# GpSimd issues the later gathers, and two more blocks of the second feed-forward load their float64 weights directly

## The chip, the cores and the metric

The program runs on one core of one Trainium2 chip. The number that counts is the device time of one execution in microseconds (us), here the median of a few runs. The core has five engines with an instruction stream each: TensorE (PE), VectorE (DVE), ScalarE (ACT), GpSimd (POOL) and SyncE (SP). SP and POOL issue the kernel's DMA transfers, each in the order of its own stream; the data are moved by 16 DMA engines which both share.

## The reference

Three stages stand one behind the other, on 1536 tokens of 384 features:

```python
# 1. gated linear attention: 2 batches, 8 heads of 48, 768 positions
state = alpha[t][:, None] * state + outer(k[t], v[t])
y[t] = q[t] @ state
# 2. top-1 mixture of experts: E = 8, F = 1024, capacity 384 rows each
expert_idx = argmax(x @ w_gate); gate_w = softmax(...)[expert_idx]
y = relu(disp @ w1[e]) @ w2[e]          # disp: the rows sent to expert e
out[i] = gate_w[i] * y[expert_idx[i], pos[i]]
# 3. second feed-forward, d_ff = 2048, weights w_in and w_out in float64
h = x @ w_in
g = h * tanh(softplus(h))
out = g @ w_out
```

## The kernel before

**Attention and routing** (0 to about 80 us). Twelve tiles of 128 tokens. At the very start SP loads the operands of the first tiles: `load_an` (L420) brings alpha, `load` (L443) brings q, k, v. Each finished tile is routed, and POOL scatters its rows into the table `tab` in DRAM (`scatter`, L108), at the place of their expert. The last two tiles are scattered last. They are also put together for expert 0 by matmuls: `slot_rest` (L834) adds for each of two chunks of rows (`CH`: 128 and 112) what expert 0's gather brought, and `route_rank_mm` stands between the two chunks.

**The experts** (82 to 223 us). The loop runs over 8 experts `e` and 8 blocks `m` of 128 hidden features: 64 steps of `g1` (L1047), and `g2` (L1064) of an earlier step. Three matmuls (high times high, low times high, high times low) make each product nearly exact in single precision, so each weight piece `st` from DRAM is split on the chip: ACT copies it to `whi` (L336), DVE subtracts to get `wlo` (L342). A piece is a block of one of the two matrices. The rows of expert e+1 are brought by `gather(e + 1)` (L124), two DMAs of 128 and 112 rows, into `xs`, which has one buffer. `xpose` (L1019) reads them by PE at m = 5 of expert e, and right behind it in the program stands the next gather. SP's queue carries the gathers, all weight pieces, and the conversion's loads and stores, one behind the other; an entry whose condition isn't met holds all behind it.

**The float64 weights.** While the experts run, 17 conversion jobs turn the weights of the first MA = 10 of 16 blocks of the second feed-forward into single precision. A job is a load of 64-bit words into `w64` (L222), an ACT square and check (L195, L230) and two DVE bit operations (`cvt_a`), a DVE join (`cvt_b`, L206) and a store to DRAM (L238), into `wi_s` or `wo_s`. Their halves lie evenly over 45 free steps (`job_at`). Later the weights are read back as pieces `st64` and on (`load_to`, L324), and `written(i)` names the jobs that must be done before a piece is loaded. The other 6 blocks are "late": `late_load` brings the 64-bit words directly (`sd`, L265 and L267), and ACT and DVE turn them into `whi` and `wlo` in some eight operations spread over the steps (`late_size`, `late_join`, `late_high`, `late_low`).

**The second feed-forward** (211 to 421 us). `f1` (L1127) and `f2` (L1170) run over 48 steps: first 10 blocks times three windows of 512 tokens, then 6 blocks times three. `f_mish(n)` has the activation, from PSUM (`sigma`, L1139 and L1143), and the sine tables (L1145), on ACT, then DVE's part. The first three steps (`EARLY`) overlap with the last three of the experts. The last piece conversions of that stretch, `conv_to`, stand on ACT behind `sigma(0)`.

Instructions on one engine run in the written order; the framework puts in the waits.

Of the kernel before, what the change touches and what calls it, by code (L numbers as in the profile page):

```python
# [10 lines left out]
F32 = mybir.dt.float32  # L11
# [12 lines left out]
def kernel(  # L24
# [18 lines left out]
    nc = tc.nc  # L43
# [3 lines left out]
    E = w1.shape[0]  # L47
# [11 lines left out]
    MF = FF // 128  # L59
    MF2 = FF2 // 128  # L60
    WIN = 240
    WB = 256
    CH = [(c, min(128, WIN - c)) for c in range(0, WIN, 128)]
    XW = NT + WIN
    PW = 768
# [13 lines left out]
    wst = main.enter_context(tc.tile_pool(name="wst", bufs=WST))  # L79
# [16 lines left out]
    tab = dram.tile([E * NT, DM], F32, name="tab")  # L96
# [23 lines left out]
    def gather(e):  # L120
        xs = xs_t[e] = xsp.tile([128, len(CH), DM], F32, tag="xs", name="xs")
        for c, n in CH:
            r0_ = (E - 1 - e) * NT + c
            r = nc.sync.dma_start(out=xs[0:n, c // 128, :], in_=tab[r0_:r0_ + n, :])  # L124
            for ins in free_rows["tab"]:
                tc.add_manual_dep(
                    r.ins, ins.name, mybir.DependencyInfo(mybir.DependencyClass.Sync, mybir.DependencyReason.DATA), reason="rows"
                )
# [30 lines left out]

    CN = 512  # L160
    MA = 10
    FH = MA * 128
    cvt_jobs = []
    wi_s = dram.tile([DM, FH], F32, name="wi_s")
    wo_s = dram.tile([FH, DM], F32, name="wo_s")
# [88 lines left out]


    late_t = {}
    NLATE = 2 * (MF2 - MA)

    def late_load(n):
        if not 0 <= n < NLATE:  # L260
            return
        st = wst.tile([128, PW], F32, tag="st", name=f"sd{n}")
        fs = slice(FH + n // 2 * 128, FH + (n // 2 + 1) * 128)
        if n % 2:
            nc.sync.dma_start(out=words(st), in_=words(w_out[fs, :]))  # L265
        else:
            nc.sync.dma_start(  # L267
                out=st.bitcast(U32).rearrange("p (k f) -> p k f", k=KD),
                in_=w_in.bitcast(U32)[:, 2 * fs.start:2 * fs.stop].rearrange("(k p) f -> p k f", p=128),
            )  # L270
        late_t[n] = st


    def late_size(n):
        if 0 <= n < NLATE:
            w = wst.tile([128, PW], F32, tag="st", name="sw")
            wt, wm = w[:, 0:DM].bitcast(U32), w[:, DM:2 * DM]
            late_t[n] = words(late_t[n]), wt, wm
            cvt_size(late_t[n][0][:, :, 1], wm)
# [6 lines left out]

    def late_at(n):
        wm = late_t[n][2]
        i = E * NP1 + (MA + n // 2) // 2 * 2 + n % 2
        if n // 2 % 2 == 0:  # L290
            if i == 76:
                early.close()
                wr_p.append(main.enter_context(tc.tile_pool(name="wr2", bufs=4, side="right")))
            w_new(i)
        if n % 2:
            hi, lo = w_second(E, MA + n // 2)
            w = wm
        else:
            hi, lo = w_first(E, MA + n // 2)
            w = wm.rearrange("p (k f) -> p k f", k=KD)  # L300
        return hi, lo, w

# [46 lines left out]
    def w_first(e, m):  # L349
        i = NP1 * e + m // 2 * 2  # L350
        return [w[i].rearrange("p (k f) -> p k f", k=KD)[:, :, m % 2 * 128:(m % 2 + 1) * 128] for w in (whi, wlo)]

    def w_second(e, m):
        i = NP1 * e + m // 2 * 2 + 1
        return [w[i][:, m % 2 * DM:(m % 2 + 1) * DM] for w in (whi, wlo)]


    with ExitStack() as actx:
# [58 lines left out]
        def load_an(i, js=range(HP)):  # L417
            if i < NTILE:
                j = slice(js.start, js.stop)
                nc.sync.dma_start(  # L420
                    out=an_b[i % 3][:, j, 1:CS], in_=alpha_t[i].rearrange("p (j c) -> p j c", j=HP)[:, j]
                )
# [17 lines left out]
        def load(into, i, src, name):  # L440
            if 0 <= i < NTILE:
                t = ld.tile([128, src.shape[2]], F32, tag=name, name=name)
                nc.sync.dma_start(out=t, in_=src[i])  # L443
                into[i] = t
# [399 lines left out]
        load(kn_t, 0, k_t, "kn")  # L844
        load_an(1)
        load(qn_t, 1, q_t, "qn")
        load(vn_t, 0, v_n, "vn")
        load(kn_t, 1, k_t, "kn")
        load_an(2)
        load(vn_t, 1, v_n, "vn")  # L850
        nc.sync.dma_start(out=sel, in_=sel_w)
        nc.sync.dma_start(out=toks.rearrange("(p c) o -> p (c o)", p=128), in_=srt)
# [131 lines left out]
        route_exp(i)  # L984
        route_idx(i)
        route_hot(i)
        slot_rest(*CH[0])
        route_rank_mm(i)
        slot_rest(*CH[1])
        route_gate(i)  # L990
        route_x(i)
        route_rank(i)
# [224 lines left out]


    def f_mish(n):
        late = (n - EARLY) // 2 if n > EARLY else -9  # L1220
        if n % 2 == 0:
            late_high(late - 1)
            sigma(at(n)) if at(n) else None
            late_size(late)
        elif at(n):
            sigma(at(n))
        if n in last_of:
            bs = [at(i) for i in last_of[n]]
            cosine(bs)
        for m, c in full:  # L1230
            (f_out if m >= MA else f_keep)(c)
        full.clear()
        now = list(due)
        due.clear()
        if n in last_of:
            due.extend(bs)
        for b in now:
            gated(b)
        if n % 2:
            late_low(late - 2)  # L1240
            late_join(late - 1)
            late_load(late + LATE_AHEAD - 1)
        conv_to(E * MF - EARLY + n + 3 + LEAD)
# [51 lines left out]
    for e in range(E):  # L1295
        for m in range(MF):
            step = e * MF + m
            if m == 6:
                off_v[e] = place(e)
            g1(e, m)  # L1300
            pend.append((e, m))
            if len(pend) > LAG:
                pe, pm = pend.pop(0)
                g2(pe, pm)
                if pm == MF - 1:
                    y_out(pe)
            if e == E - 1 and m >= MF - EARLY:
                f_head(m - MF + EARLY)
            conv_to(min(step + 1 + LEAD, ATT + step * 9 // 8))
            for f, n in job_at.get(step, ()):  # L1310
                f(n)
                if f is cvt_b:
                    cvt_load(n + 3)
            if step == 3:
                check_all(cm)
                slow_at()
            if step == 1:
                places()
            if step == 2:
                sort_places()  # L1320
            if step % 4 == 3 and 0 < step // 4 <= NTILE:
                tok_scatter(step // 4 - 1)
            if e == E - 1 and m == 0:
                nc.sync.dma_start(
                    out=srt, in_=toks.rearrange("(c p) o -> p (c o)", p=128), allow_slow_non_contiguous=True
                )
            if step == E * MF - 4:
                cvt_marks()
            if step == E * MF - 2:
                cvt_flag()  # L1330
            if m == 5 and e + 1 < E:
                xpose(e + 1)
                if e + 2 < E:
                    gather(e + 2)
# [2 lines left out]
    apart.append(at(EARLY))  # L1337
    f1(at(EARLY))
    y_out(E - 1)
    for i in range(LATE_AHEAD):  # L1340
        late_load(i)
    f_mish(EARLY)
    f_tail(EARLY)
    for n in range(EARLY + 1, NS):
# [235 lines left out]
```

## Time and profile before

| | |
|---|---|
| runs | 433.01, 427.7 and 427.75 us |
| median | 427.75 us |
| profiled execution | 429.41 us, span 427.2 us |
| mean granted TensorE clock | 0.995 |
| PE busy | 410.7 us, 96% of the span |
| DVE, ACT, POOL busy | 324.5, 327.6, 62.9 us |
| moved by DMA | 68.89 MB |

The span runs from the first to the last instruction of the profiled execution; 2.2 us of its time lie outside it. An engine is busy while it works on an instruction, so waiting shows as idle time, and a row names in brackets what ended it. For DMAs, a row of SPq shows when entries were issued; the time to landing is given apart.

### The profile page before, as it was taken

What the parts mean: (1) busy time and instruction counts of PE and PEld (TensorE: products, weight loads), DVE (VectorE), ACT (ScalarE), POOL (GpSimd) and SP (SyncE); (2) the same over time, 40 slices, a digit from 0 to 9 for tenths busy, and PEclk for the clock granted to TensorE, in tenths of its full rate; (3) what the DMA queues carried; (4) which work ended last, traced back from release to release, by engine and by line L of the source; (5) the groups of instructions that cost most, each with busy time, mean ns of one, the idle gap of its engine ahead of it and who ended that gap; (6) DMA issues with size and microseconds to landing.
All of it is one profiled execution on the core that took longest, in us unless ns stands there. A gap on an engine that the chain in (4) does not pass through costs nothing.

```text
span 427.2 us, 8408 instructions
## 1 busy us (share of the span) xinstructions
PE 410.7 (96%) x3118; PEld 375.3 (88%) x3121; DVE 324.5 (76%) x647; ACT 327.6 (77%) x579; POOL 62.9 (15%) x76
## 2 busy tenths in 40 slices
PE   7898989999999999999999999999999999999994
PEld 3797877899999989999988999898989898889893
DVE  7999987799999987988747867975796455475451
ACT  5887996688788767777688788888878878797630
POOL 5231675212012011100000000000000000003033
PEclk9999999999999999999999999999999999999998
DMA  8999995679999999996160112112000000001022
GB/s 246 340 290 335 328 364 213 218 230 281 365 309 327 349 276 343 328 298 210 58 203 0 39 45 67 38 37 76 1 1 2 0 2 0 2 1 74 2 75 79
DMA packets 51565, 68.89 MB, mean 161 GB/s; under 512 B 5500, under 2 KB 41852, under 8 KB 51516
## 3 DMA queue, kind: packets, MB, share of 16 engines
q1 hardware_dynamic: 49596, 63.55, 47.6%
q0 software_dynamic: 1920, 4.73, 3.0%
q8 instruction: 26, 0.43, 0.4%
q14 instruction: 23, 0.19, 0.1%
HBM read 56.65 MB, written 11.61 MB: 160 GB/s over the span
## 4 chain that ended last, share of the span: by engine, by line
PE 75%; DVE 11%; DMA 6%; ACT 3%; issue 3%; SPq 1%; POOL 0%; POOLq 0%; DVEq 0%; ACTq 0%
PE bk L1170 23%; PE bk L1127 23%; PE bk L1047 12%; PE bk L1064 11%; DMA w<-in_w_out_dram 2%; DMA xs<-tab 2%; DVE pt L457 2%; PE bk L519 2%; DVE wlo L342 2%; DMA an<-in_alpha_t_dram 1%; DVE q L506 1%; PE bk L565 1%; DVE rt L489 1%; PE bk L581 1%; DVE er L484 1%
## 5 line engine op out<-in xcount | busy, mean ns | idle before, releaser
L342 DVE TENSOR_TENSOR wlo<-st,whi 128x768 fp32r<-128x768 f32 x74 | 69.9, 953 | 15.5 <-ACT whi L336 14.3
L1155 DVE TENSOR_TENSOR p<-p,bk 128x512 f32<-128x512 f32 x48 | 32.8, 683 | 51.8 <-ACT p L1145 51.8
L1170 PE MATMUL bk<-whi,big 128*128 128x384 f32 x240 | 66.7, 338 | 0.8 <-DVE x2l L1074 0.8
L336 ACT ACTIVATE whi<-st 128x768 fp32r<-128x768 f32 x74 | 61.5, 841 | 0.0
L1139 ACT ACTIVATE p<-bk 128x512 f32<-128x512 f32 x48 | 28.8, 599 | 35.0 <-PE bk L1127 33.5
L1064 PE MATMUL bk<-hl,whi 128*128 128x240 f32 x192 | 52.8, 275 | 0.0
L1064 PE MATMUL bk<-hh,wlo 128*128 128x240 f32 x192 | 52.7, 274 | 0.0
L1064 PE MATMUL bk<-hh,whi 128*128 128x240 f32 x192 | 52.6, 274 | 0.0
L108 POOL DMA_INDIRECT out_dram<-acc,srt x12 | 12.2, 1017 | 232.8 <-DVE acc L1194 228.7
L1170 PEld LDWEIGHTS bk<-whi,big 128*128 128x128 f32 x240 | 44.1, 188 | 2.6 <-DVE x2l L1074 1.1
L1127 PE MATMUL bk<-x2l,whi 128*128 128x512 f32 x144 | 41.7, 397 | 0.0
L1127 PE MATMUL bk<-x2h,wlo 128*128 128x512 f32 x144 | 41.1, 394 | 0.0
L1127 PE MATMUL bk<-x2h,whi 128*128 128x512 f32 x144 | 41.0, 393 | 0.0
L1051 ACT ACTIVATE hh<-bk 128x240 fp32r<-128x240 f32 x64 | 23.5, 367 | 22.4 <-PE bk L1047 22.4
L1170 PE MATMUL bk<-wlo,big 128*128 128x384 f32 x120 | 40.6, 338 | 0.0
L1064 PEld LDWEIGHTS bk<-hl,whi 128*128 128x128 f32 x192 | 36.3, 189 | 0.2 <-DVE hl L1052 0.2
L1064 PEld LDWEIGHTS bk<-hh,whi 128*128 128x128 f32 x192 | 36.4, 189 | 0.0
L1064 PEld LDWEIGHTS bk<-hh,wlo 128*128 128x128 f32 x192 | 36.3, 189 | 0.0
L1047 PE MATMUL bk<-xh,whi 128*128 128x240 f32 x192 | 33.2, 281 | 0.6 <-ACT xh L1036 0.4
L1127 PEld LDWEIGHTS bk<-x2h,wlo 128*128 128x128 f32 x144 | 27.0, 188 | 6.7
L1127 PEld LDWEIGHTS bk<-x2l,whi 128*128 128x128 f32 x144 | 27.1, 188 | 6.3
L1145 ACT ACTIVATE p<-p,quarter 128x512 f32<-128x512 f32 x48 | 32.1, 717 | 0.3
(230 smaller groups left out, 964.3 us busy)
## 6 DMA issues: line engine op xcount, KB each, us to landing
st<-in_w_dram SPq DMA_DIRECT2D x64, 384.0 KB, 8.3
qn<-in_q_t_dram SPq DMA_DIRECT2D x12, 256.0 KB, 5.5
kn<-in_k_t_dram SPq DMA_DIRECT2D x12, 256.0 KB, 5.5
w<-in_w_in_dram SPq DMA_DIRECT2D x6, 512.0 KB, 7.1
w<-in_w_out_dram SPq DMA_DIRECT2D x6, 512.0 KB, 10.8
tab<-zero SPq DMA_DIRECT2D x4, 720.0 KB, 6.4
an<-in_alpha_t_dram SPq DMA_DIRECT2D x11, 256.0 KB, 5.7
vn<-in_v_n_dram SPq DMA_DIRECT2D x12, 192.0 KB, 4.9
```

Source lines behind the costliest of these rows:

```text
L108: r = nc.gpsimd.indirect_dma_start(out=dst[:, :], out_offset=bass.IndirectOffsetOnAxis(ap=idx, axis=0), in_=src, in_offset=None, bounds_ch ...
L336: nc.scalar.activation(out=whi[i], in_=w, func=AF.Copy)
L342: nc.vector.tensor_tensor(out=wlo[i], in0=w, in1=whi[i].bitcast(F32), op=ALU.subtract)
L457: nc.vector.tensor_tensor_scan(out=pt[0:R2, c], data0=at[0:R2, c], data1=starts[0:R2, c], initial=0.0, op0=ALU.mult, op1=ALU.add)
L1047: nc.tensor.matmul(out=hps, lhsT=a[:, kk], rhs=b_[:, kk, :], start=(n == 0), stop=(n == 3 * KD - 1))
L1051: nc.scalar.activation(out=hh, in_=hps, func=AF.Relu)
L1064: nc.tensor.matmul(out=y[n], lhsT=a[:, ns], rhs=b_, start=(m == 0 and t == 0 and n % 2 == 0), stop=(m == MF - 1 and t == 2), skip_group_ch ...
L1127: r = nc.tensor.matmul(out=hps, lhsT=a[:, kk], rhs=b_[:, kk, w0:w0 + wd], start=(n == 0), stop=(n == 3 * KD - 1))
L1139: nc.scalar.activation(out=p, in_=h2_t[b], func=AF.Sigmoid, scale=-1.0)
L1145: nc.scalar.activation(out=p_t[b], in_=p_t[b], func=AF.Sin, scale=-2.0, bias=quarter)
L1155: nc.vector.tensor_tensor(out=g, in0=g, in1=h2_t.pop(b), op=ALU.mult)
L1170: nc.tensor.matmul(out=o_t[c], lhsT=a[:, ts], rhs=b_, start=(m in (0, MA) and n == 0), stop=(m in (MA - 1, MF2 - 1) and n == 2),)
```

## The change

There are four edits.

- The gathers of experts 1 to 7 are issued by POOL and not by SP; that of expert 0 stays.
- Of the ten blocks of the first pass, eight (`MC`) are converted through DRAM: 12 jobs and 72 pieces instead of 17 and 74, over the same steps. Blocks 8 and 9 become late blocks, 16 late pieces instead of 12. The first three are loaded in steps 57 to 59 and not behind the last expert, the first six take buffers of the right-hand pool, and `late` in `f_mish` starts with n = 0.
- The third alpha tile's load goes ahead of the first v and the second k load.
- The two chunks of `slot_rest` stand together behind `route_rank_mm`.

```diff
@@ -121,7 +121,7 @@
         xs = xs_t[e] = xsp.tile([128, len(CH), DM], F32, tag="xs", name="xs")
         for c, n in CH:
             r0_ = (E - 1 - e) * NT + c
-            r = nc.sync.dma_start(out=xs[0:n, c // 128, :], in_=tab[r0_:r0_ + n, :])
+            r = (nc.gpsimd if e else nc.sync).dma_start(out=xs[0:n, c // 128, :], in_=tab[r0_:r0_ + n, :])
             for ins in free_rows["tab"]:
                 tc.add_manual_dep(
                     r.ins, ins.name, mybir.DependencyInfo(mybir.DependencyClass.Sync, mybir.DependencyReason.DATA), reason="rows"
@@ -159,7 +159,8 @@
 
     CN = 512
     MA = 10
-    FH = MA * 128
+    MC = 8
+    FH = MC * 128
     cvt_jobs = []
     wi_s = dram.tile([DM, FH], F32, name="wi_s")
     wo_s = dram.tile([FH, DM], F32, name="wo_s")
...
-    NLATE = 2 * (MF2 - MA)
+    NLATE = 2 * (MF2 - MC)
+    NRIGHT = 6
+
+    def late_pool(n):
+        return raw_p[n >= NRIGHT]
...
-        st = wst.tile([128, PW], F32, tag="st", name=f"sd{n}")
+        st = late_pool(n).tile([128, PW], F32, tag="st", name=f"sd{n}")
...
-        i = E * NP1 + (MA + n // 2) // 2 * 2 + n % 2
+        i = E * NP1 + (MC + n // 2) // 2 * 2 + n % 2
...
         load_an(1)
         load(qn_t, 1, q_t, "qn")
+        load_an(2)
         load(vn_t, 0, v_n, "vn")
         load(kn_t, 1, k_t, "kn")
-        load_an(2)
...
-        slot_rest(*CH[0])
         route_rank_mm(i)
-        slot_rest(*CH[1])
+        for c, n in CH:
+            slot_rest(c, n)
...
     def f_mish(n):
-        late = (n - EARLY) // 2 if n > EARLY else -9
+        late = (n + 1) // 2
...
+            if E * MF - EARLY - 1 - LATE_AHEAD <= step < E * MF - EARLY - 1:
+                late_load(step - (E * MF - EARLY - 1 - LATE_AHEAD))
...
     y_out(E - 1)
-    for i in range(LATE_AHEAD):
-        late_load(i)
     f_mish(EARLY)
```

On SP, behind the last gather of expert 0 (`w64` are the first three conversion loads, `st14` and on the weight pieces), there stands before:

```order
L222 DMA w64_1370<-in_w_in_dram 128x1024
L222 DMA w64_1372<-in_w_in_dram 128x1024
L222 DMA w64_1374<-in_w_in_dram 128x1024
L124 DMA xs_1387<-tab_77 128x384
L124 DMA xs_1387<-tab_77 112x384
L324 DMA st14_1416<-in_w1_dram 128x3x256
L324 DMA st15_1418<-in_w2_dram 128x2x384
L324 DMA st16_1420<-in_w1_dram 128x3x256
```

and now:

```order
L223 DMA w64_1370<-in_w_in_dram 128x1024
L223 DMA w64_1372<-in_w_in_dram 128x1024
L223 DMA w64_1374<-in_w_in_dram 128x1024
L329 DMA st14_1416<-in_w1_dram 128x3x256
L329 DMA st15_1418<-in_w2_dram 128x2x384
L329 DMA st16_1420<-in_w1_dram 128x3x256
L329 DMA st17_1422<-in_w2_dram 128x2x384
```

The two gathers of expert 1 are gone from SP, and the weight pieces follow the conversion loads directly.

On POOL, around the last scatters into the table (`toks` is the scatter of the sorted tokens' numbers), there stands before:

```order
L108 DMA tab_77<-xg_1209,si_1200 12288x384
L524 AFFINE_SELECT st__1222<-st__1222 128x512 x2
L108 DMA tab_77<-xg_l0_165,si_l0_169 12288x384
L108 DMA tab_77<-xg_l1_166,si_l1_170 12288x384
L108 DMA toks_78<-tokid_103,pos_i_104 1536x1 x12
L108 DMA out_0_dram<-acc_4040,srt_105 1536x384 x2
```

and now:

```order
L108 DMA tab_77<-xg_1209,si_1200 12288x384
L529 AFFINE_SELECT st__1222<-st__1222 128x512 x2
L108 DMA tab_77<-xg_l0_165,si_l0_169 12288x384
L108 DMA tab_77<-xg_l1_166,si_l1_170 12288x384
L124 DMA xs_1387<-tab_77 128x384
L124 DMA xs_1387<-tab_77 112x384
L124 DMA xs_1566<-tab_77 128x384
L124 DMA xs_1566<-tab_77 112x384
L108 DMA toks_78<-tokid_103,pos_i_104 1536x1 x2
L124 DMA xs_1848<-tab_77 128x384
```

The gathers of expert 1 and of expert 2 now stand ahead of the first pair of `toks` scatters, and a gather stands between each two pairs that follow.

On SP at the end of the experts (`st68` and on are the last pieces read back, `wo_s` the last stores of the conversion, `sd` the 64-bit loads of late blocks), there stands before:

```order
L324 DMA st71_3228<-wo_s_117 128x2x384
L238 DMA wi_s_116<-wt_3234 128x256
L1324 DMA srt_105<-toks_78 128x12x1
L238 DMA wo_s_117<-wt_3343 128x384
L238 DMA wo_s_117<-wt_3460 128x384
L324 DMA st72_3530<-wi_s_116 128x3x256
L324 DMA st73_3532<-wo_s_117 128x2x384
L267 DMA sd0_3685<-in_w_in_dram 128x3x256
L265 DMA sd1_3687<-in_w_out_dram 128x768
L267 DMA sd2_3689<-in_w_in_dram 128x3x256
```

and now:

```order
L329 DMA st67_3065<-wo_s_117 128x2x384
L239 DMA wo_s_117<-wt_3034 128x512
L239 DMA wo_s_117<-wt_3184 128x512
L1329 DMA srt_105<-toks_78 128x12x1
L272 DMA sd0_3352<-in_w_in_dram 128x3x256
L270 DMA sd1_3384<-in_w_out_dram 128x768
L272 DMA sd2_3412<-in_w_in_dram 128x3x256
L239 DMA wo_s_117<-wt_3346 128x512
L329 DMA st68_3480<-wi_s_116 128x3x256
L329 DMA st69_3482<-wo_s_117 128x2x384
L329 DMA st70_3484<-wi_s_116 128x3x256
L329 DMA st71_3486<-wo_s_117 128x2x384
L270 DMA sd3_3552<-in_w_out_dram 128x768
```

The last conversion store now has the four pieces `st68` to `st71` behind it, where before it had `st72` and `st73`; three late loads have moved ahead of it.

## Rows read from the trace of the kernel before

**Rows 1.** Waits of PE: engine, line, releaser: us in total, times, longest.

```profile
PE bk L1019 <- DMA xs<-tab: 1.3, 2, 0.8
...
PE bk L1170 <- DVE x2l L1074: 0.8, 1, 0.8
```

**Rows 2.** Windows: busy us (instructions) of PE, PEld, DVE, ACT, POOL; clock; DMA; GB/s.

```profile
82.00:84.00 2.00, 1.91 (x14) 1.80 (x15) 1.64 (x5) 0.54 (x2) 0.00 (x0) 1.00 1.02 412
...
152.00:162.00 10.00, 8.50 (x70) 7.69 (x70) 7.71 (x14) 7.01 (x15) 2.26 (x2) 1.00 1.03 279
```

**Rows 3.** Timeline of PE, 139 to 163: start, us, what [idle before <- releaser].

```profile
139.32 0.50 PE L1047 MATMUL bk<-xh,whi 128*128 128x240 f32 x3
...
141.35 0.78 PE L1019 MATMUL bk<-ident,xs 128*128 128x128 f32 x6
141.90 0.58 PE L1047 MATMUL bk<-xh,whi 128*128 128x240 f32 x3
...
152.05 0.50 PE L1047 MATMUL bk<-xh,whi 128*128 128x240 f32 x3
...
154.38 0.60 PE L1047 MATMUL bk<-xh,whi 128*128 128x240 f32 x3 [0.15 <-DVE hl L1052]
...
156.70 0.60 PE L1047 MATMUL bk<-xh,whi 128*128 128x240 f32 x3
...
159.83 0.55 PE L1019 MATMUL bk<-ident,xs 128*128 128x128 f32 x3 [0.85 <-DMA xs<-tab]
...
161.12 0.58 PE L1047 MATMUL bk<-xh,whi 128*128 128x240 f32 x3
```

**Rows 4.** Timeline of ACT, 150 to 156.

```profile
152.09 0.69 ACT L195 ACTIVATE wm<-w 128x512 f32<-128x512 f32 x1 [1.76 <-DMA w<-in_w_out_dram]
```

**Rows 5.** Timeline of SP's DMA queue, 140 to 163.

```profile
149.04 3.38 SPq L124 DMA_DIRECT2D xs<-tab  x2
```

**Rows 6.** Timeline of POOL, 76 to 96.

```profile
79.42 1.17 POOL L108 DMA_INDIRECT tab<-xg_l,si_l  x1 [0.30 <-issue]
88.58 1.76 POOL L108 DMA_INDIRECT toks<-tokid,pos_i  x1 [8.00 <-DVE pos_i L1110]
```

**Rows 7.** Tile xs, all its gathers.

```profile
DMA to landing us min/median/max: 2.7/8.9/11.0
```

**Rows 8.** Timeline of SP's DMA queue, 78 to 96.

```profile
78.62 1.31 SPq L222 DMA_DIRECT2D w<-in_w_in_dram  x3
86.31 0.80 SPq L124 DMA_DIRECT2D xs<-tab  x2
```

**Rows 9.** Timeline of PE, 90 to 92.

```profile
90.99 0.78 PE L1019 MATMUL bk<-ident,xs 128*128 128x128 f32 x6
```

**Rows 10.** Timeline of SP's DMA queue, 195 to 222.

```profile
204.55 6.72 SPq L238 DMA_DIRECT2D wo_s<-wt  x2
...
212.98 0.37 SPq L324 DMA_DIRECT2D st<-wo_s  x1
```

**Rows 11.** DMA issues, 203 to 222: engine, count, KB each, median us to landing.

```profile
wo_s<-wt SPq DMA_DIRECT2D x2, 192.0 KB, 1.9
...
st<-wo_s SPq DMA_DIRECT2D x1, 384.0 KB, 4.6
```

**Rows 12.** Timeline of ACT, 212 to 222.

```profile
213.61 2.30 ACT L336 ACTIVATE whi<-st 128x768 fp32r<-128x768 f32 x3
...
217.19 0.60 ACT L1139 ACTIVATE p<-bk 128x512 f32<-128x512 f32 x1 [1.03 <-PE bk L250]
```

**Rows 13.** Timeline of DVE, 212 to 229.

```profile
222.25 0.96 DVE L342 TENSOR_TENSOR wlo<-st,whi 128x768 fp32r<-128x768 f32 x1 [4.76 <-ACT whi L336]
```

**Rows 14.** Page, part 5: one group, busy us, mean ns | idle, releaser.

```profile
L342 DVE TENSOR_TENSOR wlo<-st,whi 128x768 fp32r<-128x768 f32 x74 | 69.9, 953 | 15.5 <-ACT whi L336 14.3
```

**Rows 15.** Timeline of DVE, 9 to 14.

```profile
10.32 1.23 DVE L457 TENSOR_TENSOR_SCAN pt<-an,bk 112x516 f32<-112x516 f32 x1 [0.26 <-DMA an<-in_alpha_t_dram]
```

More of the change, by code (lines that the diff above doesn't have):

```diff
@@ L275, in late_size @@
         if 0 <= n < NLATE:
-            w = wst.tile([128, PW], F32, tag="st", name="sw")
+            w = late_pool(n).tile([128, PW], F32, tag="st", name="sw")
             wt, wm = w[:, 0:DM].bitcast(U32), w[:, DM:2 * DM]
@@ L295, in late_at @@
         if n % 2:
-            hi, lo = w_second(E, MA + n // 2)
+            hi, lo = w_second(E, MC + n // 2)
             w = wm
         else:
-            hi, lo = w_first(E, MA + n // 2)
+            hi, lo = w_first(E, MC + n // 2)
             w = wm.rearrange("p (k f) -> p k f", k=KD)
```

## The prediction

> **What bounds the kernel now.** I read the page first, then PE's waits, then busy time in windows, and last the timelines around the few holes. PE is busy for 410.7 of 427.2 us (the table), so the time is PE's work plus the holes in PE's row, and an edit that leaves PE's work as it is can only open or close holes. PE's matmuls are the same before and after; only `route_rank_mm` changes place. The list of PE's waits shows few that a transfer ends: 1.3 us in two waits for a gather (`xs`), and 0.8 us for `x2l` [rows 1]. The window from 152 to 162 is where experts run and PE does least, 8.50 of 10 us with 70 matmuls [rows 2].
>
> How much is lost there is read better from the starts of steps [rows 3]. A plain step takes 2.03 us (139.32 to 141.35), and one with the transposes of the next expert's rows 2.58 (139.32 to 141.90). The steps that start at 152.05 and 154.38 take 2.33 and 2.32, and the one from 156.70 with its transposes 4.42 (to 161.12). That is 0.30 + 0.29 + 1.84 = 2.4 us lost, more than the waits view says, since a matmul whose successor waits is drawn longer.
>
> Two causes stand next to each other. ACT sat 1.76 us at 152.09 for a 64-bit load of a conversion job [rows 4], and `hh`, which the next matmuls need, stood behind it on ACT. And the gather was late: `xs` was free when the transposes of 141.35 were done (0.78 us, 142.1), but SP issued the gather only at 149.04 [rows 3, 5], 6.9 us later, with conversion loads and weight pieces ahead of it in its queue. It landed at the second chunk's transposes, after 159.83.
>
> **The gather at 142, and the conversion load at 152: minus 2.4 us.** On POOL the gather has only short `toks` scatters ahead of it. It is issued when `xs` is free, plus POOL's time to write descriptors: 1.17 us for an indirect DMA of the same size [rows 6], so about 1.2 for each chunk, and the second is out at 144.5. With the slowest landing of any gather, 11.0 us [rows 7], it is there at 155.5; it is needed at about 158.1, a period of seven plain steps and one with transposes after 141.35 (7 x 2.03 + 2.58 = 16.8). So this wait has to go. The load that ACT waited for belongs to 17 jobs in 45 steps, one about each 2.6 steps; 12 jobs in the same steps are one each 3.75 steps, and the load, issued three jobs ahead, gets about two fifths more time. 1.76 us of lateness fits in that. What is late next would be the weight pieces, which SP now issues without gathers between them. I take the whole, -2.4; the bounds are -2.4 and 0.
>
> A rule speaks against this. The trace shows the gather held 6.9 us before its issue, and then about 10 us in flight, so both the queue and the engines have a part. The Trainium skill, page "DMA: Bandwidth & Descriptors", section "Issuing engines are not separate DMA queues", says that all issuers share the same 16 DMA engines, so that issuing from more of them saves only the sequencer's time, usually a small part of a transfer. By that rule little of the hole would go; by the row the sequencer's part is no small one here, 6.9 of some 18 us, because SP's entries block each other. I follow the row, and keep the rule's result as a rival.
>
> **The first gather on POOL: plus 1.6 us.** Here the move goes the other way. Before, SP issues three 64-bit loads from 78.62 on and then stops at the gather of expert 1 until the last table scatter, issued at 79.42, has landed; it issues the gather at 86.31, and the transposes run at 90.99 without a wait [rows 6, 8, 9]. So the gather found idle DMA engines, and its landing is the smallest of all, 2.7 us for the first chunk [rows 7]. Now SP doesn't stop: it goes on with the pieces `st14` and on. POOL waits for the same scatter and then writes descriptors, so that the gather's second chunk is out at about 86.31 + 2 x 1.1 = 88.5 instead of 87.1, behind what SP has issued by then. As an estimate: three loads of 0.52 MB, four pieces at once and two more as buffers come free (0.39 MB each), and the scatters' 0.39 MB make 4.3 MB, at the 412 GB/s of the window from 82 to 84 [rows 2] 10.4 us from 80.5, so 91. The second chunk then lands at 92.5 to 93, against a need at about 91.1: 1.4 to 1.9, I take +1.6. The bounds are +0.1, if it takes the 2.7 us of rows 7 from 88.5 (91.2), and +8.4 with their 11.0 us (99.5). I take the low part because only a queue drained by 91 lies ahead, not a steady load.
>
> Behind the gather on POOL stands that of expert 2, which waits for `xs` until the transposes, and then the first `toks` scatters. These came at 88.58 [rows 6] and now start near 93. They chain on each other's landing, and the last must land only before `srt` is read in the last expert, so nobody waits for that.
>
> **The end of the conversion: plus 1.5 us.** The last store to DRAM is now job 11's, in the same step as job 16's before. SP issues the stores from 204.55 on for 6.72 us, so the last leaves at about 210.9 [rows 10], and lands 1.9 us later [rows 11], at 212.9. Before, only `st72` and `st73` depended on it, which nothing needs soon. Now `st68` to `st71` do. `st69` takes `st73`'s place in the queue: issued at 212.98, landing 4.6 us later [rows 10, 11], at 217.6. But ACT wants it at once: the three conversions of 213.61 are `whi67` to `whi69`, 2.30 us in a row [rows 12], and stand ahead of two `hh` copies and of the activation at 217.19. So `whi69` now ends at 218.4 (a third of 2.30 is 0.77) instead of 215.9, 2.5 us later, of which ACT's idle 1.03 us ahead of the activation [rows 12] takes up some: +1.5. From there the chain is unbroken, ACT's activation, tables, `whi`, then DVE from 222.25 on [rows 13], then `x2l`, for which PE waits 0.8 us already [rows 1], so a delay on ACT comes out on PE in full. Bounds: +0.7, if `st69` needs 3.8 us, twice the 1.9 of a store of half its size, and +2.5 with the two pieces `st70` and `st71` sharing the engines (393 KB at 412 GB/s is about 1 us).
>
> The first late pieces now have their square, copy and four DVE operations in this stretch. A late piece is handled in halves of the width of `wlo`, whose mean is 953 ns [rows 14], so four operations are under 3.8 us; DVE idles 4.76 us and ACT 1.03 us there [rows 12, 13]. They cost nothing with that cover, about 1 us on ACT if it is gone, which lies within the +2.5.
>
> **The rest.** The alpha tile's load is put ahead of 448 KB of others, about 1.1 us at 412 GB/s; DVE waited 0.26 us for it [rows 15]: -0.3, bounds -0.3 and +0.5 (the v or k load, now later by its 256 KB). The swap of `slot_rest` and `route_rank_mm` moves work of under 1 us within a stretch in which the next matmuls wait for ACT and DVE anyway: 0. Five conversion jobs less on ACT and DVE free these engines while PE is the bound: 0. Four more late pieces in the 48 steps of the second feed-forward come at the same rate as before and start sooner: 0.
>
> Sum: -2.4 + 1.6 + 1.5 - 0.3 = +0.4. On the profiled execution that is 429.41 to 429.8, its span 427.2 to 427.6; on the median, which is 1.66 us below that execution, 427.75 to 428.15, so **428.2 us**.
>
> **The rivals.** *Both new holes are covered (425.1).* The gather shares the engines fairly with SP's backlog and lands by 91.1, and `st69` is there in time or ACT's delay is taken up by the slack of 1.03 us [rows 12]; then only -2.4 and -0.3 are left: 427.75 - 2.7 = 425.1. For it: how the engines divide between two issuers is shown by no row, and a gather that shared them evenly would not wait for the whole backlog. Against: all gathers, of which most were issued into a loaded stretch, took 8.9 us in the median [rows 7].
>
> *The gather lands at the slowest row (435.0, slower).* From 86.3 on the first chunk is issued into weight pieces that SP keeps adding to; if the second takes 11.0 us from 88.5 [rows 7], it is there at 99.5, where 91.1 is wanted, 8.4 in place of 1.6: 428.2 + 6.8 = 435.0. It decides from a landing above some 4.5 us on. If POOL also had long issues at each of the seven gathers, some hold PE again, and the time goes on to 441. POOL's indirect issues took 1.17 and 1.76 us beside a busy DVE [rows 6], which speaks against that part. The Trainium skill, page "SBUF — State Buffer", section "A bandwidth-pool intuition that's wrong (but worth ruling out)", has a rule for it: descriptors that GpSimd writes wait while DVE holds the port both share, and a DMA of some 620 ns alone then takes some 3100. By that figure two chunks would need up to 6 us at each gather, an estimate of +4 at the first; the rows say 1.2 to 1.8.
>
> *The change doesn't reach the hole (430.6).* The gather at 142 issues early, but the same 16 engines are full (DMA share 1.03 from 152 to 162 [rows 2]), and the steps from 152 on lose the same 2.4: 427.75 + 0.4 + 2.4 = 430.6.
>
> **How the numbers follow.** The forecast, 428.2, has 0.50, with a range of its own from 426.8 to 429.8 by the bounds of single terms. Both holes covered, 425.1: 0.28. The hole stays, 430.6: 0.11. The slow gather, 435.0 and above: 0.09; the rest, 0.02, are gains I don't see. A range from 424.8 to 431 leaves out the slow gather and the rest. 2%, about what a measurement of this kernel can tell from no change, is 8.6 us: below 419.2 is faster, above 436.3 slower. Faster: 0.02; slower: 0.04, the upper half of the slow gather; same: 0.94.
>
> **What would show it.** In the profile after, PE's steps from 152 to 162 take 2.0 us and none waits for `xs`: right for the first term. PE waits 1 to 2 us for `xs` at its first transposes near 91, and SP issues pieces without a stop from 80 to 86: right for the second. ACT waits for `st` near 217 and PE a bit over 2 us for `x2l` or `hl` near 228: right for the third. I am wrong if a gather holds PE for over 3 us, if the first feed-forward shows new waits of ACT for `st`, or if the span changes where these three places don't.

## The result, and the profile after

The changed kernel takes 432.6 us (median of 15 runs, 430.24 to 433.83); the kernel before took 428.65 in the 15 runs beside it. The ratio is 1.0081, with a 95% interval from 1.0057 to 1.0104: 3.5 us slower, within 2%, and above the top of the forecast range, 431. The 15 runs of the kernel before reach from 427.03 to 433.01, and its median beside the experiments was about 1 us lower, so the experiments are set against their own. The profiled execution took 432.6 us with a span of 430.9, against 429.41 and 427.2.

On the page after, PE's busy time is what it was, 410.4 us. POOL's has grown by 7.6 us and DVE's by 5.2, ACT's has fallen by 2.8; the DMA engines moved 1.57 MB less.

```profile
PE 410.4 (95%) x3118; PEld 375.4 (87%) x3121; DVE 329.7 (77%) x650; ACT 324.8 (75%) x570; POOL 70.5 (16%) x90
...
DMA packets 49534, 67.32 MB, mean 156 GB/s; under 512 B 5372, under 2 KB 39644, under 8 KB 49484
```

So holes have moved. PE's waits after, the rows that answer to [rows 1]:

```profile
PE bk L1024 <- DMA xs<-tab: 2.5, 2, 2.2
...
PE bk L1175 <- DVE x2l L1079: 0.8, 1, 0.8
```

The waits for `xs` are there again, larger, and now the first of the list. But they are at another place, as PE's timeline shows (start, us, what, idle before and its releaser); these rows answer to [rows 3, 9]:

```profile
82.14 0.64 PE L1052 MATMUL bk<-xh,whi 128*128 128x240 f32 x3 [0.72 <-ACT xh L1041]
...
94.73 0.55 PE L1024 MATMUL bk<-ident,xs 128*128 128x128 f32 x3 [2.18 <-DMA xs<-tab]
95.58 0.51 PE L1024 MATMUL bk<-ident,xs 112*128 112x112 f32 x3 [0.30 <-DMA xs<-tab]
...
160.30 0.50 PE L1052 MATMUL bk<-xh,whi 128*128 128x240 f32 x3
162.32 0.78 PE L1024 MATMUL bk<-ident,xs 128*128 128x128 f32 x6
162.87 0.58 PE L1052 MATMUL bk<-xh,whi 128*128 128x240 f32 x3
...
231.35 0.44 PE L1175 MATMUL bk<-whi,big 128*128 128x384 f32 x1 [0.80 <-DVE x2l L1079]
```

Set against the starts of the same matmuls before, these give the account of the two profiled executions. The first matmul of the experts comes 1.3 us later (82.14 for 80.85). Up to the matmul behind the first transposes (95.85 for 91.54) 3.0 more are lost. From there to the one behind the fifth (162.87 for 161.12) 2.6 are won: the steps ahead of it take 2.0 us, and the transposes of 162.32 wait for nothing. From the last expert's last `g1` (217.04, 218.84 after) to the `f2` that waits for `x2l` (228.64, 231.35 after) 0.9 are lost, and 1.0 from there to the end, most of it behind PE's last matmul. +1.3 + 3.0 - 2.6 + 0.9 + 1.0 is 3.6 of the 3.7 us by which the spans differ. The times of the two executions differ by 3.2 only, since 1.7 us of the time lie outside the span and no longer 2.2. The prediction had no term for the end behind PE's last matmul: 0.9 us more there, less the 0.5 outside the span, leave some 0.4.

The 3.0 us are seen on POOL and SP. POOL's timeline, the answer to [rows 6], SP's queue, to [rows 8], and the landing times of all gathers, to [rows 7]:

```profile
80.70 1.49 POOL L108 DMA_INDIRECT tab<-xg_l,si_l  x1 [0.30 <-issue]
88.05 1.17 POOL L124 DMA_DIRECT2D xs<-tab  x2 [5.86 <-PE bk L778]
```

```profile
80.90 10.38 SPq L329 DMA_DIRECT2D st<-in_w_dram  x7
```

```profile
DMA to landing us min/median/max: 2.4/6.7/8.0
```

SP no longer stops between 80 and 86; from 80.90 on it issues seven pieces. POOL writes both chunks' descriptors in 1.17 us, 0.6 each and not 1.1. But the first chunk lands 6.6 us after its issue and the second 6.9, where the same gather from SP took 2.7 and 4.1, with the next pieces 0.9 us behind it in the same queue. These are the DMA issues (what, engine, count, KB each, us to landing) before, from 86 to 87.2, and after, from 87 to 90:

```profile
xs<-tab SPq DMA_DIRECT2D x1, 192.0 KB, 2.7
xs<-tab SPq DMA_DIRECT2D x1, 168.0 KB, 4.1
```

```profile
xs<-tab POOLq DMA_DIRECT2D x1, 192.0 KB, 6.6
xs<-tab POOLq DMA_DIRECT2D x1, 168.0 KB, 6.9
```

The end of the conversion shows on ACT, the answer to [rows 12]:

```profile
218.93 0.85 ACT L341 ACTIVATE whi<-st 128x768 fp32r<-128x768 f32 x1 [1.50 <-DMA st<-wo_s]
```

### The profile page after: what moved, and what is told of

It reads as the page before. It is cut to its first block, busy times and chain, and to the rows that moved or that the text cites. A ratio compares the mean times of both kernels' runs of the same rounds, so it can differ in the third digit from the quotient of the medians.

```text
span 430.9 us, 8374 instructions
## 1 busy us (share of the span) xinstructions
PE 410.4 (95%) x3118; PEld 375.4 (87%) x3121; DVE 329.7 (77%) x650; ACT 324.8 (75%) x570; POOL 70.5 (16%) x90
## 4 chain that ended last, share of the span: by engine, by line
PE 78%; DVE 10%; ACT 4%; DMA 4%; issue 2%; POOL 0%; POOLq 0%; DVEq 0%; ACTq 0%
PE bk L1175 23%; PE bk L1132 21%; PE bk L1052 14%; PE bk L1069 13%; DVE pt L462 2%; PE bk L524 2%; DMA xs<-tab 2%; DVE q L511 1%; DMA st<-wo_s 1%; PE bk L570 1%; PE bk L1024 1%; DVE rt L494 1%; DVE er L489 1%; PE bk L586 1%; PE bk L559 1%
## 5 line engine op out<-in xcount | busy, mean ns | idle before, releaser
L347 DVE TENSOR_TENSOR wlo<-st,whi 128x768 fp32r<-128x768 f32 x72 | 68.3, 955 | 15.5 <-ACT whi L341 14.0
L341 ACT ACTIVATE whi<-st 128x768 fp32r<-128x768 f32 x72 | 59.9, 840 | 2.1 <-DMA st<-wo_s 1.5
```

Of the source, the lines that this page charges most:

```text
L341: nc.scalar.activation(out=whi[i], in_=w, func=AF.Copy)
L347: nc.vector.tensor_tensor(out=wlo[i], in0=w, in1=whi[i].bitcast(F32), op=ALU.subtract)
```

## The experiments

Each was compared with runs of the kernel before on the same chip; these had medians of 427.63 (26 runs), 427.6 (30) and 427.74 (22) for the three groups in which the experiments ran. The changed kernel was not run again beside them. The first theory was the sum above: 3.0 us lost at the first gather, 0.9 at the end of the conversion, 2.4 won at 152. Its rival was that the loss lies elsewhere, in the attention stage or in POOL's issue as such.

**Only the first gather back on SP.**

```diff
-            r = (nc.gpsimd if e else nc.sync).dma_start(...)
+            r = (nc.gpsimd if e > 1 else nc.sync).dma_start(...)
```

> The changed kernel, but the gather of expert 1 is issued by SP again; those of experts 2 to 7 stay on POOL. Theory A (the first gather's move costs 3.0 us, because SP's weight pieces now go ahead of it and beside the last table scatters): the transposes near 91 don't wait for xs, ACT doesn't wait for the scatter near 85, SP stops for some 6 us near 80 to 86, and the time falls from 432.6 by 3.0 to 429.6. Rival B (most of the loss is that of the attention stage, 1.3 us, and of the end, and the gather would wait anyway): a wait for xs of over 1.5 us stays, time 431.5 to 432.6.

427.83 us (12 runs), ratio 0.999, interval 0.9957 to 1.0023. The whole loss is gone, 4.8 us against the changed kernel where 3.0 were expected. PE's timeline shows the first transposes without a wait:

```profile
90.52 0.89 PE L1024 MATMUL bk<-ident,xs 128*128 128x128 f32 x6
```

The place is right. But the version has the fifth gather on time as well. With 2.4 us won there and 0.9 lost at the end of the conversion it should be 1.5 us faster than before, and it is not.

**The conversion in fewer steps.**

```diff
-    CVT_END = 45
+    CVT_END = 38
```

> The changed kernel with its 12 conversion jobs over 38 free steps instead of 45, so that the last store is out some 8 steps earlier and st68 to st71 are there when ACT wants them. Theory A (the wait of 1.50 us on ACT for st69 costs 0.9 us on PE): ACT near 217 doesn't wait for st, 432.6 falls by 0.9 to 431.7. Rival B (the denser jobs bring the late 64-bit load back): ACT waits for w in the experts' steps, and the time stays at 432.6 or goes up to 433.5. Rival C (ACT's wait is hidden, the late blocks' own work sets the activation): ACT waits no more and the time stays within 0.3 us.

431.85 us (9 runs), ratio 1.0076 (1.004 to 1.0113). In its profile ACT's three conversions run without a wait and the activation waits for PE:

```profile
214.00 2.30 ACT L341 ACTIVATE whi<-st 128x768 fp32r<-128x768 f32 x3
216.21 0.35 ACT L1056 ACTIVATE hh<-bk 128x240 fp32r<-128x240 f32 x1
217.16 0.60 ACT L1144 ACTIVATE p<-bk 128x512 f32<-128x512 f32 x1 [0.61 <-PE bk L251]
```

The wait is gone, as theory A has it. Its number, 0.9, is only near: 0.75 us lie between the medians, which can't be told from nothing on nine runs that reach from 429.94 to 433.55. The version with both repairs, below, settles it.

**The attention's loads in the old order.**

```diff
         load(qn_t, 1, q_t, "qn")
-        load_an(2)
         load(vn_t, 0, v_n, "vn")
         load(kn_t, 1, k_t, "kn")
+        load_an(2)
```

> The changed kernel with the attention's first loads in the order of before. Theory A (the 1.3 us lost in the attention stage come from a table scatter that landed late, 7.8 us instead of 5.7, in that one execution, and not from the order of the loads): PE's first matmul of the experts comes at 80.8 or at 82.1 independent of this edit, DVE waits 0.26 us again for the third alpha tile, and the time is 432.6 to 432.9. Rival B (the order shifts the later transfers against each other): the first matmul of the experts comes at 80.9, ACT doesn't wait for the table scatter near 58, and the time is 431.3.

433.07 us (7 runs), ratio 1.01 (1.0056 to 1.0144): theory A's number, within noise, and not rival B's 431.3. The profiled execution was a long one, 436.76 us: the granted clock was 0.58 from 16 to 24 us, which put the experts' first matmul at 84.4, so that this row says nothing of the order. ACT's wait for the table scatter near 58 was not in it. In the two versions above, with the new order, the experts' first matmul stood at 80.9 and 80.7, so the 1.3 us in the attention stage are not in every execution with it. But they aren't in one alone either. ACT waits for that scatter, which landed after 7.8 us in the changed kernel and after 5.7 before, in three of the six profiles with the new order: 1.6 us in the changed kernel, 1.3 in the version with both repairs, whose experts start at 81.66, and 0.3 in the one with SP stopped until the gather has landed. In none of the seven with the old order does it. So the order may have a part in it; the times don't show a price, and the profiles are too few to tell.

**Only the gathers on POOL**, in the kernel before.

```diff
-            r = nc.sync.dma_start(...)
+            r = (nc.gpsimd if e else nc.sync).dma_start(...)
```

> The kernel before, with nothing but the gathers of experts 1 to 7 on POOL. Theory A (the move closes the gather's part of the hole at 152 to 161, 1.84 us, not the part of the 64-bit load, 0.6 us, and opens 3.0 us at the first gather): 428.65 - 1.84 + 3.0 = 429.8, with a wait for xs of about 2.5 us near 94 and ACT's wait for w near 152 still there. Rival B (the first gather is late only because of other parts of the change): no wait for xs near 91 and 426.8.

431.61 us (12 runs), ratio 1.0084 (1.0053 to 1.0115), as slow as the whole change: more than the 429.8 of theory A. The wait for `xs` is there (1.9 and 0.9 us); ACT's wait for `w` near 152 is not, against theory A. The windows (busy us of PE, PEld, DVE, ACT, POOL, then granted clock, DMA share, GB/s) show a second price of the wait:

```profile
92.00:94.00 2.00, 0.55 (x3) 0.31 (x3) 2.00 (x4) 0.00 (x0) 0.00 (x0) 1.00 1.05 298
94.00:96.00 2.00, 1.29 (x7) 1.29 (x8) 0.43 (x2) 0.67 (x2) 0.22 (x1) 0.70 1.03 310
96.00:98.00 2.00, 2.00 (x11) 2.00 (x11) 1.05 (x3) 0.71 (x3) 1.70 (x3) 0.50 0.99 346
```

PE was idle for most of 92 to 94, and then the granted clock fell to 0.50, the lower of TensorE's two levels (1.2 and 2.4 GHz). The step behind the transposes took 3.55 us (95.16 to 98.71) instead of 2.09:

```profile
95.16 0.97 PE L1047 MATMUL bk<-xh,whi 128*128 128x240 f32 x3
98.71 0.50 PE L1047 MATMUL bk<-xh,whi 128*128 128x240 f32 x3
```

The execution of the version with the old loads shows the same fall at 98 to 100, behind a wait of 3.6 us. In the changed kernel's own profile PE waited for nearly as long, 2.5 us for 2.7 here, and the clock stayed at 1.00.

The mean granted clock of each run says how common the fall is. Of the 12 runs of this version five took 429.89 to 430.23 us with 0.994 to 0.996, and seven 431.42 to 434.61 with 0.987 to 0.992; the profiled one, with the fall, is one of the seven, at 0.991. Of the changed kernel's 15 runs ten took 432.18 to 433.83 with 0.987 to 0.994, and four 430.24 to 431.35 with 0.996 to 0.998. The fifteenth is the profiled one, 432.6 at 0.997: it kept its clock and had the 1.3 us of the attention stage instead. So most runs paid the wait and some 2 us beside it, and the lower clock goes with these 2 us. In the four versions below and above whose first gather is on time and whose later ones are on POOL, 2 of 46 runs have 0.993 or less; in the changed kernel and this version 15 of 27. So the fall comes with the wait, though not with every one. Where it comes is seen in two profiles alone, this one and that with the old loads.

Two questions were left: why the 2.4 us never show, and what makes POOL's first gather late.

**The kernel before, twice more.** There is no edit.

> The kernel before once more, unchanged, for a second profile and more times. Theory A (the hole of 2.4 us at 152 to 161 belongs to the one profiled execution of 429.4 us and not to the usual one of 427.0 to 427.8): PE takes 2.0 us for each of the steps there, no wait for xs, and the profiled execution takes 427 to 427.8 with a span near 425.5. Rival B (the hole is in every execution, and the changed kernel lost elsewhere what it gained there): steps of over 2.3 us and a wait for xs at the fifth transposes are there again.

> The kernel before, unchanged, one look, to see an execution of the usual time. Theory A (the hole at 152 to 161 is there only in the executions above 429 us): if this execution takes 427 to 427.8, its steps from 152 to 161 take 2.01 and 2.57 us. Rival B (the hole is always there): the steps lose 1.4 to 2.4 us again at whatever time.

427.49 us (12 runs) and one run of 429.14. Neither profile caught an execution of the usual time: they are of 430.18 and 429.14 us, and both lose time up to the fifth transposes. PE's timeline of the 429.14 execution:

```profile
152.63 0.50 PE L1047 MATMUL bk<-xh,whi 128*128 128x240 f32 x3
155.20 0.61 PE L1047 MATMUL bk<-xh,whi 128*128 128x240 f32 x3 [0.40 <-DVE hl L1052]
157.52 0.60 PE L1047 MATMUL bk<-xh,whi 128*128 128x240 f32 x3
160.24 0.83 PE L1019 MATMUL bk<-ident,xs 128*128 128x128 f32 x6 [0.43 <-DMA xs<-tab]
160.84 0.59 PE L1047 MATMUL bk<-xh,whi 128*128 128x240 f32 x3
```

It loses 0.56 + 0.31 + 0.75 = 1.6 us there, and with 429.14 - 1.6 = 427.5 it would be a usual execution. The 430.18 one waits for `xs` alone, 0.9 us at 143 and 1.2 at 161. The expectations made the question depend on the time of the execution, and no profile was of 427, so this alone settles nothing. All three profiled executions of this kernel are long ones, though three in four of its runs are not; whether the profile itself has a part in that was not tested.

**Only the gathers of experts 2 to 7 on POOL**, in the kernel before.

```diff
-            r = nc.sync.dma_start(...)
+            r = (nc.gpsimd if e > 1 else nc.sync).dma_start(...)
```

> The kernel before with the gathers of experts 2 to 7 alone on POOL; expert 1's stays on SP, 17 conversion jobs. Theory A (these gathers cost nothing and only take away the waits for xs of the slower executions; the rest of those executions' loss is elsewhere): the median is 427.0 to 427.6, within 0.2 per cent of before, the transposes wait for xs nowhere. Rival B (the gathers' move alone gives what the version with both repairs gained): 426.9, with one in ten or fewer above 429. Rival C (POOL delays gathers in general): waits for xs show at later experts and the time is above 428.

427.39 us (12 runs), ratio 0.9989 (0.9968 to 1.0011). PE's timeline has no hole at 152:

```profile
152.06 0.50 PE L1047 MATMUL bk<-xh,whi 128*128 128x240 f32 x3
154.07 0.50 PE L1047 MATMUL bk<-xh,whi 128*128 128x240 f32 x3
156.09 0.50 PE L1047 MATMUL bk<-xh,whi 128*128 128x240 f32 x3
158.11 0.78 PE L1019 MATMUL bk<-ident,xs 128*128 128x128 f32 x6
158.66 0.58 PE L1047 MATMUL bk<-xh,whi 128*128 128x240 f32 x3
```

This is the answer, and theory A. The profiled execution took 426.83 us. Its steps from the first to the last expert take 133.6 us, where the first profile of the kernel before has 136.2; up to the first expert, and from the last one to PE's last matmul, the two agree within 0.1 us. So the edit closes the hole and costs nothing elsewhere that could hide the gain. Yet the median moves by 0.1%, 0.5 us; at the interval's end 0.3%, 1.4 us. 2.4 us would be 0.56%. So the usual execution of the kernel before does not have that hole.

**Only the two blocks loaded directly**, in the kernel before (the change's edits from `MC` to `late_load`, without the other three).

> The kernel before with nothing but the two blocks loaded directly (12 conversion jobs, 16 late pieces); all gathers on SP, the loads and the rank matmul in the old places. Theory A (this part costs the 0.3 to 1.0 us at the end of the conversion and gives nothing back in the usual execution): 427.63 + 0.3 to 1.0 = 427.9 to 428.6, with ACT's wait for st near 217. Rival B (fewer jobs free the DMA engines and SP, and the time falls): 426.5 or less.

428.05 us (12 runs), ratio 1.001 (0.998 to 1.0041): within theory A's range, though the interval takes in no change at all. In its profiled execution, of 427.29 us, PE waits for no gather, with all gathers on SP. ACT waits for `st` at the end of the conversion, 0.97 us:

```profile
214.00 0.84 ACT L341 ACTIVATE whi<-st 128x768 fp32r<-128x768 f32 x1 [0.97 <-DMA st<-wo_s]
```

**SP stopped as before.** Leaving the gather on POOL, a small DMA was put on SP behind the first three 64-bit loads.

```diff
     gather(1)
+    hold = const.tile([1, 8], F32, name="hold")
+    r = nc.sync.dma_start(out=hold, in_=tab[0:1, 0:8])
+    for ins in free_rows["tab"]:
+        tc.add_manual_dep(r.ins, ins.name, ...)
```

> The changed kernel with one small DMA of 32 bytes added on SP behind the first three 64-bit loads. It reads a place of the table that no one uses, and like the gather it waits for the last table scatter, so that SP stops where it stopped before, while the gather of expert 1 is still issued by POOL. Theory A (the gather lands late because of the weight pieces that SP issues ahead of and beside it): it lands some 3 us after its issue, PE waits at most 1 us for it, and the time is 428.5 to 429.5. Rival B (POOL's issue itself is slow, by its descriptors or by its queue): the wait of 2 us or more stays, and the time is 431 to 433.

432.19 us (7 runs), ratio 1.01 (1.0063 to 1.0137), rival B's number. PE waits as long as in the changed kernel. But SP's queue shows that the experiment didn't do what its expectation took for granted:

```profile
85.43 0.25 SPq L1295 DMA_DIRECT2D hold<-tab  x1
85.79 4.49 SPq L329 DMA_DIRECT2D st<-in_w_dram  x7
```

SP and POOL are released by the same landing. SP issues its next piece at 85.79, and POOL, with its own run of waits ahead, the gather at 86.21. The backlog ahead of the gather was gone, the pieces beside it were not, and the first chunk landed 6.4 us after its issue:

```profile
xs<-tab POOLq DMA_DIRECT2D x1, 192.0 KB, 6.4
```

**SP stopped until the gather has landed.**

```diff
     gather(1)
+    hold = dram.tile([1, 2, 4], F32, name="hold")
+    nc.sync.dma_start(out=hold, in_=xs_t[1][0:1, :, 0:4])
```

> The changed kernel with one small DMA of 32 bytes added on SP behind the first three 64-bit loads, which reads what the gather of expert 1 has brought. SP so issues no weight piece until that gather has landed. Theory A (the pieces on the same 16 DMA engines hold the gather up, both ahead of it and mixed with it): it lands 3.5 to 4.5 us after its first issue, PE waits for xs by 0.5 us or less, and the time is below 430 unless the pieces, now 4 us late, make ACT wait for st some steps on. Rival B (POOL's own path is slow even with idle engines): it lands over 6 us after its issue and PE waits 2 us or more.

427.22 us (10 runs), ratio 0.9982 (0.9949 to 1.0016). The DMA issues of its stretch from 86 to 92, with KB and us to landing, and the first transposes:

```profile
xs<-tab POOLq DMA_DIRECT2D x1, 192.0 KB, 3.3
xs<-tab POOLq DMA_DIRECT2D x1, 168.0 KB, 2.9
```

```profile
90.43 0.78 PE L1024 MATMUL bk<-ident,xs 128*128 128x128 f32 x6
```

On engines that move nothing else POOL's gather lands in 3.3 us, against 2.7 from SP, and PE doesn't wait. Theory A holds and rival B falls: it is the weight pieces beside the gather that make it 6.6 us. The pieces, issued at 90.93 where the kernel before issued them at 87.21, made PE wait nowhere in the steps that follow.

**Both repairs**: the first gather on SP and `CVT_END = 38`, in the changed kernel.

> The changed kernel with the gather of expert 1 on SP and the conversion jobs over 38 steps: the two repairs together. Theory A (they add): 427.83 - 0.2 to 0.9 = 427.0 to 427.6, the lowest executions at 426.5 to 427, and hardly any execution above 430, since the hole at 152 can't come back; against the kernel before 427.63 within 0.3 per cent. Rival B (the denser jobs make the 64-bit loads late, since SP stops for the gather again): ACT waits for w, 428 or more.

426.88 us (12 runs, 426.64 to 429.24), ratio 0.9975, interval 0.9951 to 1.0. This is the fastest version tried, 5.7 us below the changed kernel and about 0.7 below the one before, at the edge of what can be told. Against the version with the first gather on SP alone (427.83), which differs from it by `CVT_END` only, it is 0.95 us faster, and nine of its twelve runs are below the lowest of the other's, 427.25: the end of the conversion does cost about 0.9 us.

## Why the prediction was wrong

The forecast was 428.2 us and 432.6 was measured, 4.4 us more. Two steps of the sum failed, the gain of 2.4 us and the price of the first gather.

**The gain of 2.4 us at 152 to 161: the first step that failed.** The mechanism was right for the execution that was shown: with the gather on POOL neither the transposes nor the steps before them wait, here or in any of the eight other versions profiled with the later gathers on POOL (nor, in one profile, with 12 jobs and all gathers on SP). What was wrong was to take 2.4 us off the median. The profiled execution stood at 429.41 us, 1.66 above the median, and the prediction carried that difference along as an offset, "the median, which is 1.66 us below that execution". It should have asked what the 1.66 us were. All three profiled executions of the kernel before took over 429 us, and the steps from the first to the last expert lost 2.5, 2.9 and 2.0 us more in them than in the profile of the version with only the later gathers moved; without that they would be at 426.9 to 427.3, the usual time. The experiment with the later gathers alone shows what the term is worth in the median, 0.1% with an interval of -0.3 to +0.1%. Beside the result itself 8 of the 15 runs of the kernel before were above 428.2, so there it may have been worth more, up to the 1 us by which that median is higher. Why some executions have the hole and others don't was not found, nor was an execution of 427 us of the kernel before seen in a profile.

**The first gather: the second step that failed, and the larger.** The place and the cause were right, the size was too small. The forecast was +1.6, with bounds from 0.1 to 8.4. Measured in the profile: 3.0 us. In runs it is more: 4.8 between the changed kernel and the one with this gather back on SP, and 4.2 between the versions with all and with only the later gathers on POOL (431.61 and 427.39). I had let the gather wait for the backlog that SP had issued by 88.5, drained at 91, "not a steady load". The stop that waited for the table showed that the backlog ahead isn't needed for it: pieces issued in the same microsecond do as much, and SP goes on adding them. And POOL's 0.6 us per chunk were cheaper than the 1.1 assumed, so the descriptors were not the cause. The Trainium skill's rule that I had weighed, page "DMA: Bandwidth & Descriptors", section "Issuing engines are not separate DMA queues", names the mechanism: both issuers share the same engines and interleave. The rows agree, 3.3 us alone and 6.6 us beside the pieces. The other rule, of descriptors that wait for DVE, from the Trainium skill's page "SBUF — State Buffer", section "A bandwidth-pool intuition that's wrong (but worth ruling out)", would give long issues on POOL. The row shows 1.17 us for both chunks beside a DVE busy for 1.93 of 2 us, so it did not decide here.

The part that I left out altogether is the clock: a change that leaves PE's work as it is, I wrote, "can only open or close holes". In two of the executions profiled the granted clock fell to 0.50 behind the wait, and the next step cost 1.5 us more in one and 1.1 in the other. Most runs of the changed kernel have the lower mean clock, at some 2 us more than those that kept it. As an estimate: the runs that kept their clock have medians of 430.5 us (the changed kernel) and 430.2 (only the gathers on POOL), 2.7 and 2.8 above the versions that differ from these by the first gather on SP; the others lie 2 higher again. So the wait is some 2.7 and the clock some 2. The rival with the slow gather had the mechanism that decided, a gather that lands far later than 2.7 us, at 435.0 with a chance of 0.09; what came lies between it and the forecast.

**The end of the conversion: the mechanism right, the size too large.** Forecast +1.5, with ACT's wait for `st69`; measured 0.9 in the profile and 0.75 to 0.95 between medians, and ACT waits 1.50 us for it. The fewer steps take it away. I had the late blocks' square and conversion as covered, and they were.

**The alpha load and the matmuls' order: near nothing, as forecast, so far as the times can tell.** The 1.3 us lost in the attention stage of the profile are seen, smaller, in one other execution with these edits, and whether the loads' order brings them stays open. DVE's 0.26 us can't be told in the times.

So with the terms as measured in runs, about +4.5 for the first gather, +0.8 for the end of the conversion and -0.4 for the later gathers, the forecast would have been some 4.9 us above a usual 427.6: 432.5, where 432.6 was measured. (These terms come from the same runs, so this shows that they add up, not that they are right.) Of the 4.4 us between forecast and result the first gather is some 2.9 and the missing gain 2.0; the end of the conversion, sized 0.7 too high, takes a part of that back. The range failed since I had let a gain that was not there pay for the first gather, and sized that gather by a backlog that drains.

## What to carry to other kernels

Before a hole in a profile is put into a sum, ask whether the profiled execution is a usual one; if its time is above the median by about the hole, the hole is the difference and not a gain to be had. Moving a transfer to another issuer takes away its wait in the old queue, but also the order that the queue gave: where the old issuer's stop kept the engines free for an urgent transfer, let it stop still, or leave that one transfer where it is. And a wait on TensorE may cost more than its length: here the step behind one of 2.7 us cost 1.5 more, at half the granted clock.

## What was not expected of the hardware

- A chunk of a gather, 192 KB, took 2.7 us from SP with weight pieces issued 0.9 us behind it in the same queue, 3.3 us from POOL on idle DMA engines, and 6.4 to 6.6 us from POOL when weight pieces were issued within half a microsecond of it or ahead of it.
- After waits of 2.7 and 3.6 us in which TensorE was nearly idle the granted clock fell to 0.50 in two executions, and it stayed at 1.00 in three others after 2.5, 2.6 and 2.7 us (the changed kernel, the one with 38 steps, the one with SP's first stop). What decides was not found.
- The profiled executions of the kernel before took 429.14, 429.41 and 430.18 us, while three in four of its 78 runs beside the experiments were below 428.2. Of the 20 longer runs 13 had a mean granted clock of 0.987 to 0.989, at 430.5 to 432.1 us; none of the three profiles is of that kind.
